# Gates of the last two tiles and x of the last loaded early, the last tiles' ends shared by ACT and DVE, and the last weight block's products put last

## The chip, the cores and the metric

The kernel runs on one core of one Trainium2 chip. The metric is the device time of one execution in microseconds (us); a number quoted for a kernel is the median of its runs. The trace of a kernel is one profiled execution; its span (first to last instruction) was 1.73 to 1.95 us shorter than the time of the same run.

Engines, as this kernel uses them (instructions on the page of the kernel before): PE multiplies matrices into PSUM banks (4674), ACT applies functions of one input (791), DVE does elementwise work on one or two inputs (833), POOL issues most loads and does a few small operations (80), SP issues transposes and the last outputs. PEld is PE's weight load (4674).

## The reference, cut to what matters

```python
xn = layernorm(x)                                   # x: (1, 2048, 448), bf16
s = attention(xn, k_cache, v_cache, wq) @ wo        # 16 heads of 256, 8 K/V heads, window 512
g = silu((gelu(xn @ w_gate) * (xn @ w_up)) @ w_down)
out = x + s * g
```

The kernel cuts the 2048 rows into 16 tiles of 128 rows, t = 0 to 15, in four chunks of four. It computes the gates g of all tiles early and parks them in DRAM (`g2d`, twice the gate: hence the factor 0.5 below). Attention then goes chunk by chunk. Each tile ends with "s times gate, plus x, write out". The ends of tiles 0 to 11 run under the attention of the following chunk. The ends of tiles 12 to 15 come when nothing else is left: this is the tail, which the change is about.

## The kernel before

A helper records operations with the buffers that they read and write and derives all semaphore waits from these. It gives each engine and each DMA issuer its list in program order, and makes a write to a buffer wait until the buffer's last readers are done.

```python
NG2 = 2      # places for gates: g2[:, t % 2]
NXR = 3      # places for x:     xr[:, t % 3]; the result is added into the same place and written out from it
CUT = D - P  # 320: tile 15 is done in two pieces, columns 0:320 and 320:448

def wo_mm(t4, b, c0=0, c1=D):                  # last four blocks (28 to 31) of s @ wo, added into the bank
    mms([(bank[b][:, c0:c1], oT[:, i, t4 * P:(t4 + 1) * P], wo[:, i - NCO + NL, c0:c1], False, i == NCO - 1)
         for i in range(NCO - NL, NCO)], b_oT[NCO - NL:] + [b_wo], (b_ps[b],))

# turn(t4, b, c0, c1): products with the identity bring the other blocks' sums into the same bank   [cut]

def wo_end(t, c0, c1, mult, bt, y):
    x, g = t % NXR, t % NG2
    bx = [b_xr[x][i] for i in range(2) if (c0 < CUT, c1 > CUT)[i]]
    mult(g2[:, g, :], b_g2[g])
    if t + NG2 < NT and c1 == D:
        load_g2(t + NG2)                       # DMA issued by POOL
    add("dve", xr[:, x, c0:c1], y[:, c0:c1], xr[:, x, c0:c1], bt + bx, bx)
    dma("sp" if t >= NT - 4 else "pool", out_view[:, t, c0:c1], xr[:, x, c0:c1], bx, ())
    if t + NXR < NT and c1 == D:
        dma("pool", xr[:, x, :], x_view[:, t + NXR, :], (), b_xr[x])

def wo_fin(c, t4, b, c0=0, c1=D):              # end of a tile of the last chunk
    ...                                        # [cut]
    def mult(g, bg):                           # tmp is 32 bit
        K.op("dve", lambda e: e.scalar_tensor_tensor(
            out=tmp[:, s, c0:c1], in0=bank[b][:, c0:c1], scalar=0.5, in1=g[:, c0:c1],
            op0=ALU.mult, op1=ALU.mult), (b_ps[b], bg), bt)
    wo_end(t, c0, c1, mult, bt, tmp[:, s, :])

# the program's end
ends = [(0, AB[2], 0, D), (1, AB[3], 0, D), (2, AB[0], 0, D), (3, AB[1], 0, CUT), (3, BB[0], CUT, D)]
for t4, b, c0, c1 in ends[:3]:
    turn(t4, b, c0, c1)
for i, (t4, b, c0, c1) in enumerate(ends):
    if i >= 3:
        turn(t4, b, c0, c1)
    wo_mm(t4, b, c0, c1)
    wo_fin(c, t4, b, c0, c1)
```

The softmax here doesn't subtract the row's maximum and nothing guards it: scores larger than these inputs give would overflow.

Of the kernel before, what the change touches and what calls it, by code (L numbers as in the profile page):

```python
# [5 lines left out]
ACT = mybir.ActivationFunctionType  # L6
ALU = mybir.AluOpType
# [161 lines left out]
def bass_recurrent_scan__sliding_block_cached__geglu_ffn__prompt_kernel(  # L169
# [12 lines left out]
    _, S, D = A_x.shape  # L182
# [5 lines left out]
    NT = S // P  # L188
# [4 lines left out]
    NCO = HD // P  # L193
# [7 lines left out]
    CUT = D - P  # L201
# [9 lines left out]
    with es:  # L211
        K = Plan(nc, es)
        base = [(nc.sbuf_base + 31) // 32 * 32]

        def place(name, shape, dt, at=None):
            size = {BF16: 2, F16: 2, F32: 4}[dt]
            for n in shape[1:]:
                size *= n
            size = (size + 31) // 32 * 32
            if at is None:  # L220
                at = base[0]
                base[0] += size
            assert at + size <= nc.sbuf_usable_end, (name, at + size, nc.sbuf_usable_end)
            return nc.alloc_sbuf_tensor_at(name, list(shape), dt, offset=at), at, at + size

        def sbuf_bufs(at, size, n):
            return [K.buf(at + i * size, size) for i in range(n)]
# [27 lines left out]
        NG2 = 2  # L255
        g2, a, _ = place("g2", [P, NG2, D], BF16)
        b_g2 = sbuf_bufs(a, D * 2, NG2)
        g2d = nc.dram_tensor("g2_all", [NT, P, D], BF16)
        b_g2d = [K.buf() for t in range(NT)]
# [7 lines left out]
        NXR = 3  # L267
        xr, a, _ = place("xr", [P, NXR, D], BF16)
        b_xr = [[K.buf(a + (i * D + lo) * 2, (hi - lo) * 2) for lo, hi in ((0, CUT), (CUT, D))] for i in range(NXR)]
        tmp, a, _ = place("tmp", [P, 2, QC], F32)  # L270
        b_tmp = [[K.buf(a + (i * QC + lo) * 4, (hi - lo) * 4) for lo, hi in ((0, CUT), (CUT, QC))] for i in range(2)]

        tmpb, _, _ = place("tmpb", [P, 2, 2 * QC], BF16, at=a)
# [10 lines left out]
        NL = 4  # L284
        wo, a, a2 = place("wo", [P, NL, D], BF16, at=rw + WAT[0] * Hq * N2 * 2)
        assert NL * D <= Hq * N2
        b_wo = K.buf(a, NL * D * 2)
# [34 lines left out]
        b_oT = sbuf_bufs(a, QC * 2, NCO)  # L322
# [8 lines left out]
        b_cc = [[K.buf(a_c + (i * 2 + j) * HC * 4, HC * 4) for j in range(2)] for i in range(4)]  # L331
        g2w, a_s, a2 = place("g2w", [P, 4, D], BF16, at=at)
        b_g2w = sbuf_bufs(a_s, D * 2, 4)
        sT, _, at = place("sT", [P, 4, 3, P], BF16, at=at)
        b_sT = [K.buf(a_s, 12 * P * 2) for k in range(3)]
        b_xs = [K.buf() for k in range(4)]
# [5 lines left out]
        bank = [pall[i // 2][:, (i % 2) * 512:(i % 2) * 512 + 512] for i in range(8)]  # L342
        b_ps = [K.buf() for i in range(8)]

        x_view = A_x.rearrange("b (t p) d -> p (b t) d", p=P)
        out_view = out.rearrange("b (t p) d -> p (b t) d", p=P)
# [8 lines left out]
        def dma(q, o, i, reads=(), writes=()):  # L355
            K.op(q, lambda e, o=o, i=i: e.dma_start(o, i), reads, writes, dma=True)  # L356
# [4 lines left out]
        def act(o, i, func, reads, writes, scale=1.0):  # L361
            K.op("act", lambda e, o=o, i=i: e.activation(o, i, func, scale=scale), reads, writes)  # L362

        def add(eng, o, x, y, reads, writes, op=ALU.add):
            K.op(eng, lambda e: e.tensor_tensor(o, x, y, op), reads, writes)  # L365

        def mms(lst, reads, writes, after=()):
            def fn(e):
                ins = None
                for (o, l, r, st, sp) in lst:  # L370
                    ins = e.matmul(o, lhsT=l, rhs=r, start=st, stop=sp, skip_group_check=True)  # L371
                return ins
            return K.op("pe", fn, reads, writes, after=after)
# [10 lines left out]
        def load_wr(q, i, j):  # L384
# [14 lines left out]
            out=ident[:, :], in_=ident[:, :], compare_op=ALU.not_equal, fill=1.0, base=0,  # L399
# [350 lines left out]
                    K.op("dve", lambda v, i=i, b=b, o=o, f=f: v.tensor_scalar(  # L750
                        o[:, i, :], bank[b], f, None, op0=ALU.mult), (b_ps[b],), (b_oT[i],))

        def wo_mm(t4, b, c0=0, c1=D):

            mms([(bank[b][:, c0:c1], oT[:, i, t4 * P:(t4 + 1) * P], wo[:, i - NCO + NL, c0:c1], False, i == NCO - 1)
                 for i in range(NCO - NL, NCO)], b_oT[NCO - NL:] + [b_wo], (b_ps[b],))

        def turn(t4, b, c0=0, c1=D):

            tok = slice(t4 * P, (t4 + 1) * P)  # L760
            lst = [(0, 0, tok, slice(0, P)), (P, 2, tok, HALF[0]), (N2, 1, tok, slice(0, P)), (N2 + P, 2, tok, HALF[1]),
                   (2 * N2, 3, slice(t4 % 2 * P, t4 % 2 * P + P), HALF[t4 // 2])]
            lst = [x for x in lst if c0 <= x[0] < c1]
            mms([(bank[b][:, lo:lo + k.stop - k.start], xs[j][:, q], ident[:, k], i == 0, False)
                 for i, (lo, j, q, k) in enumerate(lst)], b_xs + [b_ident], (b_ps[b],))

        def wo_end(t, c0, c1, mult, bt, y):

            x, g = t % NXR, t % NG2
            bx = [b_xr[x][i] for i in range(2) if (c0 < CUT, c1 > CUT)[i]]  # L770
            mult(g2[:, g, :], b_g2[g])
            if t + NG2 < NT and c1 == D:
                load_g2(t + NG2)
            add("dve", xr[:, x, c0:c1], y[:, c0:c1], xr[:, x, c0:c1], bt + bx, bx)
            dma("sp" if t >= NT - 4 else "pool", out_view[:, t, c0:c1], xr[:, x, c0:c1], bx, ())
            if t + NXR < NT and c1 == D:
                dma("pool", xr[:, x, :], x_view[:, t + NXR, :], (), b_xr[x])

        def load_g2(t):
            dma("pool", g2[:, t % NG2, :], g2d[t], (b_g2d[t],), (b_g2[t % NG2],))  # L780

        def wo_fin(c, t4, b, c0=0, c1=D):
            t = c * 4 + t4
            s = t % 2
            bt = [b_tmp[s][i] for i in range(2) if (c0 < CUT, c1 > CUT)[i]]

            def mult(g, bg):
                K.op("dve", lambda e: e.scalar_tensor_tensor(  # L788
                    out=tmp[:, s, c0:c1], in0=bank[b][:, c0:c1], scalar=0.5, in1=g[:, c0:c1],
                    op0=ALU.mult, op1=ALU.mult), (b_ps[b], bg), bt)  # L790
            wo_end(t, c0, c1, mult, bt, tmp[:, s, :])

        o_view = oTh.rearrange("p (h e) (r q) -> p e r h q", e=2, r=2)
        HALF = (slice(0, R), slice(R, P))
# [111 lines left out]
        def burst_end(c, t4):  # L906
            t = c * 4 + t4
            s, u = t % 2, t4 // 2
            y = tmpb[:, s, 0:D]

            def mult(g, bg):
                two = lambda x, lo, hi: x[:, 0:2 * N2].rearrange("p (n d) -> p n d", n=2)[:, :, lo:hi]
                for at, i, reads in ((lambda x: two(x, 0, P), sT[:, t4, 0:2, :], b_sT[:2]),
                                     (lambda x: two(x, P, N2), sT[:, t4, 2, :].rearrange("p (n d) -> p n d", n=2), b_sT[2:]),
                                     (lambda x: x[:, 2 * N2:D], sN[:, t4 % 2, u * R:u * R + R], [b_sN])):
                    add("dve", at(y), i, at(g), reads + [bg], b_tmp[s], ALU.mult)
            wo_end(t, 0, D, mult, b_tmp[s], y)
# [7 lines left out]
        for m in range(NS):  # L925
            if m in groups:
                hi = groups[groups.index(m) + 1]
# [34 lines left out]
        ends = [(0, AB[2], 0, D), (1, AB[3], 0, D), (2, AB[0], 0, D), (3, AB[1], 0, CUT), (3, BB[0], CUT, D)]  # L962
        for t4, b, c0, c1 in ends[:3]:
            turn(t4, b, c0, c1)
        for i, (t4, b, c0, c1) in enumerate(ends):
            if i >= 3:
                turn(t4, b, c0, c1)
            wo_mm(t4, b, c0, c1)
            wo_fin(c, t4, b, c0, c1)

        K.schedule()
# [53 lines left out]
```

## Time and profile before

| quantity | before |
|---|---|
| time, median of the first 3 runs (of 4, with one more beside the changed kernel) | 557.06 us (556.98 us) |
| span of the profiled run | 554.6 us |
| PE busy | 543.2 us (98%) |
| first turning product of the tail (start S) | 540.85 us |
| end of DVE's last add | 552.45 us |

The page's first part gives busy time, share of the span and number of instructions; its second part gives the busy share in 40 slices, in tenths. These are its line for all engines and its slices of PE, of the kernel before:

```profile
PE 543.2 (98%) x4674; PEld 295.0 (53%) x4674; DVE 361.3 (65%) x833; ACT 312.6 (56%) x791; POOL 41.1 (7%) x80
PE   9999999999999999999999999999999999999993
```

PE is at least 90% busy in every slice but the last. The share of 98% thus hides the end: PE's last product ends at 545.46, and others work for another 9 us. The chain of waits of that stretch (start, duration, what; lines of code by number) shows what it consists of, in the kernel before:

```profile
543.02 0.64 DVE tmp L788
...
543.94 2.48 DMA g<-g_all
...
546.51 0.64 DVE tmp L788
...
547.31 0.44 POOL xr L356
...
547.84 2.97 DMA g<-g_all
...
550.90 0.50 DVE tmp L788
...
552.16 0.29 DVE xr L365
```

The gate of tile 14 is loaded only when tile 12's multiply has freed its place. The gate of tile 15 is issued by POOL at 547.84, behind POOL's load of x for tile 15 at 547.31. The two gate loads alone are 5.45 us of the chain. The waits of that stretch (engine, output and line, what it waited for: us in all, times, longest) say the same:

```profile
DVE tmp L788 <- DMA g<-g_all: 4.1, 2, 3.1
POOL xr L356 <- DVE tmp L788: 2.8, 1, 2.8
```

The second line names a DVE multiply as what the x load waited for. The code has no such dependence: the x load takes the place that tile 12's *output* is read from, so it waits for that output to land.

The groups of instructions by form show what the arithmetic costs. First the ends in the tail, then the ends of tiles 0 to 11, which are done in 16 bit, both of the kernel before:

```profile
L788 DVE SCALAR_TENSOR_TENSOR tmp<-bank,g 128x448 f32<-128x448 f32 x3 | 1.9, 623 | 2.0 <-PE bank L371 1.0 <-DMA g<-g_all 1.0
L365 DVE TENSOR_TENSOR xr<-tmp,xr 128x448 bf16<-128x448 f32 x3 | 1.9, 625 | 0.1
```

```profile
L365 DVE TENSOR_TENSOR xr<-tmpb,xr x12: 391/392/393, 250.1 to 494.9; 128x448 bf16<-128x448 bf16 x12
```

In the tail a multiply takes 623 ns and an add 625 ns. The same add from 16-bit operands takes 392 ns (the second fence has minimum, median and maximum in ns).

### The profile page before, as it was taken

The page shows a single profiled execution, that of the slowest core. Times are in us where ns is not written, and L with a number is a line of the kernel's source. Part 1 is how long each engine was busy: PE and PEld are TensorE (multiplying, and loading weights), DVE is VectorE, ACT ScalarE, POOL GpSimd, SP SyncE. Part 2 cuts the span into 40 slices and gives each one's busy share as a digit, 9 for nine tenths or more (in the row PEclk, how much of TensorE's full clock was granted, in tenths as well). Part 3 has the DMA queues.
Part 4 walks back from the last instruction along what each step waited for, and adds up shares of the span by engine and source line. Part 5 has one row for each costly group of instructions (what it writes and reads, how often), then busy time and mean ns, then how long its engine had stood idle before and what let it go on. Part 6 is the DMA issues. An engine that isn't in the chain of part 4 may idle for free.

```text
span 554.6 us, 11965 instructions
## 1 busy us (share of the span) xinstructions
PE 543.2 (98%) x4674; PEld 295.0 (53%) x4674; DVE 361.3 (65%) x833; ACT 312.6 (56%) x791; POOL 41.1 (7%) x80
## 2 busy tenths in 40 slices
PE   9999999999999999999999999999999999999993
PEld 5554444445444444974444489444446954444781
DVE  6664635663447758856766795487578746767854
ACT  5434536763548768037857831687586058858320
POOL 1141500000000000003001000300100012010001
PEclk9999999999999999999999999999999999999997
DMA  9566399903316826424853840387176026846602
GB/s 293 127 183 143 83 274 285 157 16 91 83 32 138 154 49 155 45 31 112 155 113 85 158 95 11 75 163 161 37 152 144 7 46 153 144 84 146 125 1 60
DMA packets 177001, 63.29 MB, mean 114 GB/s; under 512 B 159808, under 2 KB 173648, under 8 KB 176944
## 3 DMA queue, kind: packets, MB, share of 16 engines
q1 hardware_dynamic: 172960, 52.76, 45.4%
q0 software_dynamic: 3216, 9.18, 5.8%
q8 instruction: 37, 0.61, 0.5%
q10 hardware_dynamic: 768, 0.57, 0.3%
q14 instruction: 20, 0.16, 0.1%
HBM read 20.22 MB, written 3.67 MB: 43 GB/s over the span
## 4 chain that ended last, share of the span: by engine, by line
PE 91%; DMA 3%; DVE 3%; ACT 2%; issue 1%; POOL 0%; DVEq 0%; POOLq 0%; ACTq 0%
PE bank L371 91%; DMA pT<-pn 2%; ACT p L724 1%; DMA g<-g_all 1%; DVE pn L731 1%; DMA x<-in_A_x_dram 0%; DVE tmp L788 0%; DVE rden L728 0%; DVE xnT L365 0%; DVE stats L418 0%; PE bank L469 0%; DVE oT L750 0%; ACT cc L362 0%; DVE xr L365 0%; DVE sr L365 0%
## 5 line engine op out<-in xcount | busy, mean ns | idle before, releaser
L724 ACT ACTIVATE p<-bank 128x512 f32<-128x512 f32 x256 | 150.5, 595 | 24.6 <-DVE pn L731 19.2
L371 PE MATMUL bank<-pT,va 128*128 128x512 bf16 x512 | 120.8, 379 | 0.4 <-DMA pT<-pn 0.4
L371 PE MATMUL bank<-kT,qT 128*128 128x512 bf16 x512 | 121.0, 379 | 0.0
L731 DVE TENSOR_SCALAR pn<-p,rden 128x512 bf16<-128x512 f32 x256 | 113.0, 484 | 9.6 <-DMA pT<-pn 5.4
L371 PE MATMUL bank<-xnT,wq 64*128 64x512 bf16 x768 | 94.9, 376 | 0.0
L371 PE MATMUL bank<-xnT,wgu 64*128 64x512 bf16 (+2 forms) x768 | 84.0, 350 | 0.1
L371 PEld LDWEIGHTS bank<-kT,qT 128*128 128x128 bf16 x512 | 49.4, 98 | 62.0 <-issue 3.8
L371 PEld LDWEIGHTS bank<-pT,va 128*128 128x128 bf16 x512 | 49.7, 98 | 61.3 <-DMA pT<-pn 2.0
L362 ACT ACTIVATE qT<-bank 128x512 bf16<-128x512 f32 x76 | 44.1, 596 | 53.2 <-PE bank L371 51.6
L709 DVE CAST qT<-bank 128x512 bf16<-128x512 f32 x52 | 35.1, 692 | 43.7 <-PE bank L371 43.7
L371 PEld LDWEIGHTS bank<-xnT,wq 64*128 64x128 bf16 x768 | 36.7, 94 | 46.3 <-ACT p L724 1.7
L371 PEld LDWEIGHTS bank<-xnT,wgu 64*128 64x128 bf16 x768 | 37.0, 94 | 36.9 <-issue 0.7
L537 DVE TENSOR_TENSOR actT<-bank,gl 128x512 bf16<-128x512 f32 x56 | 37.8, 690 | 26.5 <-PE bank L371 19.9
L362 ACT ACTIVATE gl<-bank 128x512 bf16<-128x512 f32 x56 | 33.2, 597 | 37.1 <-PE bank L371 35.0
L728 DVE RECIPROCAL rden<-rsum 128x2 f32<-128x2 f32 x128 | 21.2, 165 | 48.6 <-ACT p L724 48.4
L724 ACT ACTIVATION_READ_ACCUMULATOR p<-bank 128x1 f32 x256 | 51.4, 201 | 0.0
L371 PE MATMUL bank<-wd,actT 128*128 128x448 bf16 x224 | 43.0, 353 | 0.0
L750 DVE TENSOR_SCALAR oTh<-bank 128x512 f16<-128x512 f32 x62 | 42.4, 684 | 0.0
L371 PE MATMUL bank<-sr,wt 128*64 128x256 f16 x744 | 41.5, 273 | 0.2 <-DVE sr L365 0.2
L371 PEld LDWEIGHTS bank<-sr,wt 128*64 128x64 f16 x744 | 40.1, 110 | 1.1 <-DVE sr L365 0.5
L362 ACT ACTIVATE xnT<-bank 128x256 bf16<-128x256 f32 (+2 forms) x12 | 4.9, 417 | 63.2 <-PE bank L371 62.6
L356 POOL DMA_DIRECT2D g<-g_all x16 | 8.6, 538 | 410.6 <-DVE tmpb L365 387.3
(65 smaller groups left out, 427.3 us busy)
## 6 DMA issues: line engine op xcount, KB each, us to landing
wtb<-in_A_wo_dram POOLq DMA_DIRECT2D x4, 768.0 KB, 7.3
wq<-in_A_wq_dram SPq DMA_DIRECT2D x2, 1536.0 KB, 10.8
va<-in_A_v_cache_dram SPq DMA_DIRECT2D x8, 256.0 KB, 5.2
pT<-pn SPq DMA_TRANSPOSE x128, 2.8
g_all<-g2w SPq DMA_DIRECT2D x16, 112.0 KB, 2.0
xr<-in_A_x_dram POOLq DMA_DIRECT2D x16, 112.0 KB, 2.3
g<-g_all POOLq DMA_DIRECT2D x16, 112.0 KB, 2.3
wd<-in_B_w_down_dram SPq DMA_DIRECT2D x1, 1568.0 KB, 7.3
```

The costliest lines, as they stand in the source:

```text
L356: K.op(q, lambda e, o=o, i=i: e.dma_start(o, i), reads, writes, dma=True)
L362: K.op("act", lambda e, o=o, i=i: e.activation(o, i, func, scale=scale), reads, writes)
L371: ins = e.matmul(o, lhsT=l, rhs=r, start=st, stop=sp, skip_group_check=True)
L537: K.op("dve", lambda e: e.tensor_tensor(actT[:, c % 2, f, :], bank[b + 1], gl[:, s, :], ALU.mult), (b_ps[b + 1], b_gl[s]), (b_actT[c % 2][ ...
L709: K.op("dve", lambda v, s=s, b=b: v.tensor_copy(qT[:, s, 1, :], bank[b + 1]), (b_ps[b + 1],), (b_qT[s][1],))
L724: K.op("act", lambda e, b=b, r=r, z=z: e.activation(p32[:, z, :], bank[b], ACT.Exp, scale=att_scale, accum_out=rsum[:, r:r + 1]), (b_ps[b] ...
L728: K.op("dve", lambda e, r=r: e.reciprocal(rden[:, r - 1:r + 1], rsum[:, r - 1:r + 1]), b_rsum[r - 1:r + 1], b_rden[r - 1:r + 1])
L731: K.op("dve", lambda e, r=r - 1 + t, z=(n - 1 + t) % NP32, y=y, t=t: e.tensor_scalar(pn[:, y, t, :], p32[:, z, :], rden[:, r:r + 1], None, ...
L750: K.op("dve", lambda v, i=i, b=b, o=o, f=f: v.tensor_scalar(o[:, i, :], bank[b], f, None, op0=ALU.mult), (b_ps[b],), (b_oT[i],))
```

## The change

It has three parts.

1. **Early loads.** The gates of tiles 14 and 15 and x of tile 15 get places of their own, in a region that is free once tile 11's end is done.
2. **Ends by ACT and DVE.** For tiles 13 to 15, ACT copies the bank to a 16-bit tile (with the factor 0.5), and DVE multiplies and adds in 16 bit. Tile 12 stays as it was.
3. **Order of the products.** Blocks 28 to 30 of tiles 12 and 13 come first; block 31, whose input is ready last (PE waits 0.43 us for it in the kernel before), follows for both.

```diff
+        b_gz = sbuf_bufs(a_s, D * 2, 2)
+        b_xz = [K.buf(a_s + (2 * D + lo) * 2, (hi - lo) * 2) for lo, hi in ((0, CUT), (CUT, D))]
 ...
-        def wo_mm(t4, b, c0=0, c1=D):
+        def wo_mm(t4, b, c0=0, c1=D, lo=NCO - 4, hi=NCO):
 ...
         def wo_end(t, c0, c1, mult, bt, y):
-            x, g = t % NXR, t % NG2
+            x, bx = (xr[:, t % NXR, :], b_xr[t % NXR]) if t < NT - 1 else (g2w[:, 2, :], b_xz)
+            g, bg = (g2[:, t % NG2, :], b_g2[t % NG2]) if t < NT - 2 else (g2w[:, t % 2, :], b_gz[t % 2])
 ...
-            if t + NG2 < NT and c1 == D:
+            if t + NG2 < NT - 2:
                 load_g2(t + NG2)
 ...
+            if t == NT - 5:
+                K.reuse(b_gz + b_xz)
+                for i in range(2):
+                    dma("pool", g2w[:, i, :], g2d[NT - 2 + i], (b_g2d[NT - 2 + i],), (b_gz[i],))
+                dma("pool", g2w[:, 2, :], x_view[:, NT - 1, :], (), b_xz)
 ...  (in wo_fin)
             def mult(g, bg):
+                if t4 == 0:
+                    ...            # as before, 32 bit
+                    return
+                act(y[:, c0:c1], bank[b][:, c0:c1], ACT.Copy, (b_ps[b],), bt, scale=0.5)
+                add("dve", y[:, c0:c1], y[:, c0:c1], g[:, c0:c1], bt + [bg], bt, ALU.mult)
 ...  (at the end)
+        for t4, b, c0, c1 in ends[:2]:
+            wo_mm(t4, b, c0, c1, NCO - NL, NCO - 1)
         for i, (t4, b, c0, c1) in enumerate(ends):
 ...
-            wo_mm(t4, b, c0, c1)
+            wo_mm(t4, b, c0, c1, NCO - 1 if i < 2 else NCO - NL)
```

More of the change, by code (lines that the diff above doesn't have):

```diff
@@ L751, in pv @@
                         o[:, i, :], bank[b], f, None, op0=ALU.mult), (b_ps[b],), (b_oT[i],))
-        def wo_mm(t4, b, c0=0, c1=D):
+        def wo_mm(t4, b, c0=0, c1=D, lo=NCO - 4, hi=NCO):
             mms([(bank[b][:, c0:c1], oT[:, i, t4 * P:(t4 + 1) * P], wo[:, i - NCO + NL, c0:c1], False, i == NCO - 1)
-                 for i in range(NCO - NL, NCO)], b_oT[NCO - NL:] + [b_wo], (b_ps[b],))
+                 for i in range(lo, hi)], b_oT[lo:hi] + [b_wo], (b_ps[b],))
         def turn(t4, b, c0=0, c1=D):
@@ L767, in wo_end @@
         def wo_end(t, c0, c1, mult, bt, y):
-            x, g = t % NXR, t % NG2
-            bx = [b_xr[x][i] for i in range(2) if (c0 < CUT, c1 > CUT)[i]]
-            mult(g2[:, g, :], b_g2[g])
-            if t + NG2 < NT and c1 == D:
-                load_g2(t + NG2)
-            add("dve", xr[:, x, c0:c1], y[:, c0:c1], xr[:, x, c0:c1], bt + bx, bx)
-            dma("sp" if t >= NT - 4 else "pool", out_view[:, t, c0:c1], xr[:, x, c0:c1], bx, ())
-            if t + NXR < NT and c1 == D:
-                dma("pool", xr[:, x, :], x_view[:, t + NXR, :], (), b_xr[x])
+            x, bx = (xr[:, t % NXR, :], b_xr[t % NXR]) if t < NT - 1 else (g2w[:, 2, :], b_xz)
+            g, bg = (g2[:, t % NG2, :], b_g2[t % NG2]) if t < NT - 2 else (g2w[:, t % 2, :], b_gz[t % 2])
+            bx = [bx[i] for i in range(2) if (c0 < CUT, c1 > CUT)[i]]
+            mult(g, bg)
+            if t + NG2 < NT - 2:
+                load_g2(t + NG2)
+            add("dve", x[:, c0:c1], y[:, c0:c1], x[:, c0:c1], bt + bx, bx)
+            dma("sp" if t >= NT - 4 else "pool", out_view[:, t, c0:c1], x[:, c0:c1], bx, ())
+            if t + NXR < NT - 1:
+                dma("pool", xr[:, t % NXR, :], x_view[:, t + NXR, :], (), b_xr[t % NXR])
+            if t == NT - 5:
[3 more added lines that the diff above has]
+                dma("pool", g2w[:, 2, :], x_view[:, NT - 1, :], (), b_xz)
         def load_g2(t):
@@ L785, in wo_fin @@
             bt = [b_tmp[s][i] for i in range(2) if (c0 < CUT, c1 > CUT)[i]]
+            if t4:
+                y = tmpb[:, s, 0:D] if c0 == 0 else tmpb[:, s, CUT:CUT + D]
             def mult(g, bg):
-                K.op("dve", lambda e: e.scalar_tensor_tensor(
-                    out=tmp[:, s, c0:c1], in0=bank[b][:, c0:c1], scalar=0.5, in1=g[:, c0:c1],
-                    op0=ALU.mult, op1=ALU.mult), (b_ps[b], bg), bt)
-            wo_end(t, c0, c1, mult, bt, tmp[:, s, :])
+                if t4 == 0:
+                    K.op("dve", lambda e: e.scalar_tensor_tensor(
+                        out=tmp[:, s, c0:c1], in0=bank[b][:, c0:c1], scalar=0.5, in1=g[:, c0:c1],
+                        op0=ALU.mult, op1=ALU.mult), (b_ps[b], bg), bt)
+                    return
+                act(y[:, c0:c1], bank[b][:, c0:c1], ACT.Copy, (b_ps[b],), bt, scale=0.5)
+                add("dve", y[:, c0:c1], y[:, c0:c1], g[:, c0:c1], bt + [bg], bt, ALU.mult)
+            wo_end(t, c0, c1, mult, bt, tmp[:, s, :] if t4 == 0 else y)
         o_view = oTh.rearrange("p (h e) (r q) -> p e r h q", e=2, r=2)
```

## The prediction

> **What bounds the kernel.** The page gives a span of 554.6 us with PE busy 543.2 us (98%); the chain that ended last is 91% PE. Only the end is not: PE's slices show 9 but for the last (3). Timeline: PE's last product starts at 545.1, yet DVE works until 552.45, and the span ends 2.1 us later (last output's landing 1.5). The chain of waits from 543 us: multiply of tile 12 (0.64), gate load of tile 14 (2.48), multiply (0.64), POOL's x load issue (0.44), gate load of tile 15 (2.97), last multiplies and adds. The gate loads wait for the multiplies of tiles 12 and 13 to free their places, the second also behind the x load on POOL. DVE stands 1.0 and 3.1 us for them.
>
> **What the change does.**
> 1. *Early loads.* Gates 14, 15 and x of 15 go to a region free after tile 11's end (about 495 us), some 50 us ahead. No load is left in the tail. Alone: 543.0 + 3x1.25 (whole tiles) + 1.55 (last, in two pieces) = about 548.3 instead of 552.45: -4.1 us.
> 2. *Tiles 13 to 15 via ACT.* Now a DVE multiply out of PSUM takes 0.62 and the add with a 32-bit operand 0.62 (128x448). The 16-bit add in the earlier ends (128x448) takes 0.391. [...] So a whole tile costs DVE 0.78, not 1.25; the last pieces about 2x0.32 + 2x0.22 (estimates from 16-bit operations of 64, 128 and 448 columns), not 1.55. Saved: 3x0.47 = 1.4 us. ACT copies (256 columns 0.38, 512 columns 0.58, so about 0.54 for 448) run under DVE's previous tile; ACT is idle there.
> 3. *Last weight block last.* PE waits 0.43 us for the last oT at 541.6 to 542.05; six products (0.19 each) fill it. But tile 12's end then comes behind tile 13's first three: 543.1 instead of 542.99. PE ends 0.4 us earlier, for which nothing waits: DVE ends last. Worth 0, or -0.1 us of gain.
>
> **Sum.** Tile 12 to 544.4; 13 to 545.2; 14 to 546.0; 15 to 547.2. DVE ends 5.3 us earlier. Four outputs then leave within 3 us instead of 8, so the last may land 0 to 0.4 us slower. All of it is on the chain that ends last; the 540 us before don't change. Three POOL issues of 0.54 us move to 495 us, where PE waits for no POOL.
>
> **Time:** 557.06 - 5.2 = about 551.8 us, range 550.9 to 552.9. (-0.9%): faster by over 2% 1%, within 2% 98%, slower 1%.
>
> **What the profile would show.** No gate or x load after 520 us; DVE without a wait for a DMA in the tail; DVE end at about 547; multiplies and adds of 0.39, copies of 0.54; PE no longer waiting for oT; tile 12's multiply starting at 543.1, not earlier; the last output landing in 1.5 to 2 us. The PE stretch up to 541 us the same within 0.3 us.
>
> **What would make it wrong.** ACT's turn-around (buffers reused by parity: tile 14's copy waits for tile 12's add, tile 15's for tile 13's) becoming the chain: up to +0.6. Outputs bunching: +0.5. The early loads disturbing the transposes at 495 us: small. A different chip: 0.5.

Estimate from the trace: the multiply of a copied tile would take the 0.39 us of the 16-bit add, hence 0.78 us a tile. The sum puts DVE's end at 547.2 instead of 552.45, the 5.3 us, of which 5.2 were forecast for the time. What bunched outputs, the early loads or another chip might cost are guesses that no run had shown.

## The result, and the profile after

The changed kernel takes 551.42 us (4 runs, 550.95 to 552.08) against 556.98 us (4 runs of the kernel before). The ratio is 0.990, with a 95% interval from 0.9883 to 0.9918. A ratio in this document is the mean time of one kernel's runs over that of the other's of the same rounds, so not quite the ratio of the quoted medians. The time fell by 5.56 us between the medians, where 5.2 us was forecast.

DVE and ACT in the tail, from the timeline of the changed kernel, with SP's issue of the last two outputs (other rows are left out). A row gives start, us, engine, line, operation, output and inputs, count, idle time before and what ended it; line numbers are 2 to 11 higher than before:

```profile
544.02 0.62 DVE L799 SCALAR_TENSOR_TENSOR tmp<-bank,g 128x448 f32<-128x448 f32 x1 [0.99 <-PE bank L373]
544.21 0.54 ACT L364 ACTIVATE tmpb<-bank 128x448 bf16<-128x448 f32 x1 [1.94 <-PE bank L373]
544.68 0.62 DVE L367 TENSOR_TENSOR xr<-tmp,xr 128x448 bf16<-128x448 f32 x1
545.22 0.39 DVE L367 TENSOR_TENSOR tmpb<-tmpb,g 128x448 bf16<-128x448 bf16 x1
545.34 0.54 ACT L364 ACTIVATE tmpb<-bank 128x448 bf16<-128x448 f32 x1 [0.59 <-DVE xr L367]
545.64 0.39 DVE L367 TENSOR_TENSOR xr<-tmpb,xr 128x448 bf16<-128x448 bf16 x1
545.95 0.39 DVE L367 TENSOR_TENSOR tmpb<-tmpb,g2w 128x448 bf16<-128x448 bf16 x1
546.07 0.60 ACT L364 ACTIVATE tmpb<-bank 128x320 bf16<-128x320 f32 x2 [0.19 <-DVE xr L367]
546.37 0.39 DVE L367 TENSOR_TENSOR xr<-tmpb,xr 128x448 bf16<-128x448 bf16 x1
546.68 0.32 DVE L367 TENSOR_TENSOR tmpb<-tmpb,g2w 128x320 bf16<-128x320 bf16 x1
547.04 0.33 DVE L367 TENSOR_TENSOR g2w<-tmpb,g2w 128x320 bf16<-128x320 bf16 x1
547.28 0.22 DVE L367 TENSOR_TENSOR tmpb<-tmpb,g2w 128x128 bf16<-128x128 bf16 x1
547.39 0.90 SPq L358 DMA_DIRECT2D out_dram<-g2w  x2
547.53 0.23 DVE L367 TENSOR_TENSOR g2w<-tmpb,g2w 128x128 bf16<-128x128 bf16 x1
```

From 544.02 on DVE goes from one operation to the next without a stop. The waits for gate loads are gone, and no gate or x load is left in the tail: POOL issues the two gates at 499.31 and x of tile 15 right after, at 500.61 (the row of the gates, from POOL's timeline of the changed kernel):

```profile
499.31 1.30 POOL L358 DMA_DIRECT2D g2w<-g_all  x2
```

Each 16-bit step costs 0.39 us where a 32-bit one cost 0.62.

The starts of the tails are not equal. In the 14 profiled runs, S (the first turning product) lies between 540.85 and 542.58 us, although these kernels run the same instructions up to there, apart from three loads. The difference of 1 us between the two profiles here is built up over the whole run: the first output left at 250.9 and 251.5 us, the last early one at 495.7 and 496.5. So a span is a poor witness for a change of a few tenths, and the tails are measured from S. "DVE end" is the end of DVE's last add:

| kernel | S | DVE end after S | span's end after DVE end | sum |
|---|---|---|---|---|
| before | 540.85 | 11.60 | 2.15 | 13.75 |
| changed, first profile | 541.89 | 5.87 | 2.54 | 8.41 |
| changed, second profile (another chip) | 542.58 | 5.87 | 2.45 | 8.32 |

Spans are printed to 0.1 us, so the last two columns are good to about 0.05. The tail is 5.34 to 5.43 us shorter, which accounts for the measured 5.56 us within the scatter of the runs.

### The profile page after: what moved, and what is told of

Read it like the earlier page. It is cut to its first block, busy times and chain, and to the rows that moved or that the text cites. A ratio compares the mean times of both kernels' runs of the same rounds, so it can differ in the third digit from the quotient of the medians.

```text
span 550.3 us, 11945 instructions
## 1 busy us (share of the span) xinstructions
PE 540.5 (98%) x4649; PEld 294.7 (54%) x4674; DVE 360.0 (65%) x833; ACT 314.2 (57%) x795; POOL 41.4 (8%) x80
## 4 chain that ended last, share of the span: by engine, by line
PE 91%; DMA 2%; DVE 2%; ACT 2%; issue 1%; SPq 0%; ACTq 0%; DVEq 0%
PE bank L373 91%; ACT p L726 2%; DMA pT<-pn 2%; DVE pn L733 1%; DMA x<-in_A_x_dram 1%; DVE rden L730 0%; DVE tmpb L367 0%; SPq L358 0%; DVE qT L711 0%; DVE stats L420 0%; DVE tmp L799 0%; DVE sr L367 0%; DVE oTh L752 0%; ACT qT L364 0%; DVE g2w L367 0%
## 5 line engine op out<-in xcount | busy, mean ns | idle before, releaser
L373 PE MATMUL bank<-kT,qT 128*128 128x512 bf16 x487 | 117.8, 379 | 2.3 <-ACT qT L364 1.0
```

Source lines behind the costliest of these rows:

```text
L373: ins = e.matmul(o, lhsT=l, rhs=r, start=st, stop=sp, skip_group_check=True)
```

## The experiments

Twelve kernels were run in four groups, each beside runs of the kernel before on the same chip, with five rounds (three in the last group). All gave correct results.

| kernel | median, us | before, same rounds | ratio (95%) | S | DVE end after S | span's end after that | sum |
|---|---|---|---|---|---|---|---|
| loads_only | 552.74 | 557.19 | 0.9926 (0.9914 to 0.9938) | 541.54 | 7.29 | 2.17 | 9.46 |
| act_only | 556.72 | 557.19 | 0.9990 (0.9976 to 1.0003) | 541.12 | 10.66 | 2.52 | 13.18 |
| order_only | 557.06 | 557.19 | 0.9997 (0.9985 to 1.0010) | 541.49 | 11.59 | 2.22 | 13.81 |
| after_no_order | 551.84 | 557.19 | 0.9908 (0.9895 to 0.9922) | 541.42 | 6.14 | 2.54 | 8.68 |
| swap_only | 555.02 | 557.23 | 0.9949 (0.9934 to 0.9964) | 541.28 | 9.64 | 2.18 | 11.82 |
| after_again | 552.71 | 557.23 | 0.9908 (0.9891 to 0.9925) | 542.58 | 5.87 | 2.45 | 8.32 |
| t12_16bit_actq | 551.31 | 557.23 | 0.9885 (0.9866 to 0.9905) | 541.60 | 5.64 | 2.26 | 7.90 |
| pool_add13_actq | 552.25 | 557.23 | 0.9903 (0.9886 to 0.9919) | 541.45 | 6.27 | 2.88 | 9.15 |
| t12_16bit | 552.03 | 557.21 | 0.9909 (0.9895 to 0.9922) | 542.38 | 5.64 | 2.58 | 8.22 |
| last_whole | 551.40 | 557.21 | 0.9897 (0.9884 to 0.9911) | 541.86 | 5.49 | 2.45 | 7.94 |
| own_places_actq | 551.21 | 557.01 | 0.9887 (0.9870 to 0.9905) | 542.13 | 5.64 | 2.13 | 7.77 |
| loads_order | 552.58 | 557.01 | 0.9919 (0.9901 to 0.9936) | 540.87 | 7.26 | 2.17 | 9.43 |

### Each part alone

**loads_only** keeps part 1 and undoes the others:

```diff
 # against the changed kernel
-                act(y[:, c0:c1], bank[b][:, c0:c1], ACT.Copy, (b_ps[b],), bt, scale=0.5)
-                add("dve", y[:, c0:c1], y[:, c0:c1], g[:, c0:c1], bt + [bg], bt, ALU.mult)
+                ...                        # scalar_tensor_tensor out of the bank for all tiles [cut]
-        for t4, b, c0, c1 in ends[:2]:
-            wo_mm(t4, b, c0, c1, NCO - NL, NCO - 1)
 ...                                       # wo_mm takes all four blocks again [cut]
```

> Only the early loads of gates 14, 15 and x of 15; the ends still by DVE out of PSUM in 32 bit, products in the old order. Theory A (the late loads were the tail's chain): DVE without a wait for a DMA, one whole tile every 1.20 us as in the kernel before (543.02 to 544.22), so DVE's end moves from 552.45 to about 548.2 on the clock of before, time 3.9 to 4.3 us lower, about 552.9. Rival B (the arithmetic of the ends is what the tail waits for): gain at most 5.56 - 1.4 from multiplies and adds, but with most of the rest already lost to outputs bunching, under 3 us.

The tail's sum fell from 13.75 to 9.46 us, DVE's end by 4.31 us, and the ratio of 0.9926 is 4.1 us. Theory A's forecast held and rival B's "under 3 us" did not. DVE's rows of tile 14 and the first piece of 15 show an unbroken pace, at a step of 1.19 us (546.10 to 547.29); between tiles 12 and 13 of the kernel before it was 1.20:

```profile
546.10 0.62 DVE L796 SCALAR_TENSOR_TENSOR tmp<-bank,g2w 128x448 f32<-128x448 f32 x1
546.75 0.62 DVE L367 TENSOR_TENSOR xr<-tmp,xr 128x448 bf16<-128x448 f32 x1
547.29 0.48 DVE L796 SCALAR_TENSOR_TENSOR tmp<-bank,g2w 128x320 f32<-128x320 f32 x1
```

**act_only** is the kernel before with the changed kernel's `wo_fin` alone:

```diff
 # against the kernel before, in wo_fin; tile 12 keeps the 32-bit multiply [cut]
+                act(y[:, c0:c1], bank[b][:, c0:c1], ACT.Copy, (b_ps[b],), bt, scale=0.5)
+                add("dve", y[:, c0:c1], y[:, c0:c1], g[:, c0:c1], bt + [bg], bt, ALU.mult)
```

> Only the ends of tiles 13 to 15 by ACT and DVE in 16 bit, loads as late as before. Theory A: the last gate load still lands about 7.8 us after the start of tile 12's multiply (550.81 against 543.02 before), since it stands behind the x load that waits for tile 12's output; only the last tile's arithmetic after it shortens, 1.55 to about 0.95 us: time 0.5 to 0.7 us lower, about 556.4. Rival B (savings add up independently): the whole 1.4 us of DVE work comes off, about 555.6.

The medians differ by 0.47 us and the ratio's interval includes 1; the tail's sum fell by 0.57 us. That is theory A's size, and less than half of rival B's 1.4. The interval alone would not decide: its lower end, 0.9976, is a gain of 1.3 us. The trace does. DVE finishes tile 14 at 547.54 and then stands for three microseconds:

```profile
547.15 0.39 DVE L365 TENSOR_TENSOR xr<-tmpb,xr 128x448 bf16<-128x448 bf16 x1
550.58 0.33 DVE L365 TENSOR_TENSOR tmpb<-tmpb,g 128x320 bf16<-128x320 bf16 x1 [3.03 <-DMA g<-g_all]
```

Here time saved ahead of a wait for a DMA mostly lengthened the wait: tile 14 ended 0.52 us sooner after S than in the kernel before, but the last gate load left only 0.06 us sooner. (DVE's end itself came 0.94 us earlier, because this run's last gate load also landed faster, in 2.43 instead of 2.97 us, and the end after DVE was 0.37 us longer. The work after that load fell by 0.35 us, from 1.55 to 1.20, and not by the 0.6 expected. That the sum lies in theory A's range is thus in part luck; that the wait took up the rest is not.)

**order_only** is the kernel before with part 3 alone:

```diff
 # against the kernel before; wo_mm's new arguments [cut]
+        for t4, b, c0, c1 in ends[:2]:
+            wo_mm(t4, b, c0, c1, NCO - NL, NCO - 1)
-            wo_mm(t4, b, c0, c1)
+            wo_mm(t4, b, c0, c1, NCO - 1 if i < 2 else NCO - NL)
```

> Only the last weight block's products last. Theory A: PE ends 0.4 us earlier but tile 12's multiply starts at the same time within 0.1 us after the turning products, and with it all loads: time the same within 0.2 us (below what timing can resolve). Rival C (PE's wait for oT delays the tail): 0.4 us lower.

DVE's end after S is 11.59 against 11.60 us, and the time's interval holds 1. PE's wait for oT (0.43 us in the kernel before) is gone, but nothing came of it. Theory A held.

### Is the order worth anything inside the whole change?

**after_no_order** is the changed kernel without part 3 (the lines of order_only's diff taken away).

> The changed kernel with the products in the old order: Theory A: PE waits 0.4 us for oT again, but DVE's end relative to the first turning product is the same within 0.1 us (5.9 us), time about 551.4 to 551.7. Rival C: 0.4 us slower than the changed kernel, DVE's end at 6.3 us after the first turning product.

This is where the prediction's third step fails. DVE's end is at 6.14 us after S instead of 5.87: the order is worth 0.27 us here, outside the 0.1 us that theory A allowed. Rival C's 0.4 us is not reached either. ACT and DVE from the timeline of after_no_order show where it goes:

```profile
544.25 0.62 DVE L367 TENSOR_TENSOR xr<-tmp,xr 128x448 bf16<-128x448 f32 x1
544.35 0.54 ACT L364 ACTIVATE tmpb<-bank 128x448 bf16<-128x448 f32 x1 [2.54 <-PE bank L373]
544.92 0.39 DVE L367 TENSOR_TENSOR tmpb<-tmpb,g 128x448 bf16<-128x448 bf16 x1
...
545.17 1.29 ACT L364 ACTIVATE tmpb<-bank 128x448 bf16<-128x448 f32 x3 [0.27 <-PE bank L373]
545.35 0.39 DVE L367 TENSOR_TENSOR xr<-tmpb,xr 128x448 bf16<-128x448 bf16 x1
```

S is 541.42 here. Tile 13's copy starts 2.93 us after S; in the changed kernel it starts at 2.32 (544.21 - 541.89). So the copy ends at 544.89, and DVE, whose add ends at 544.87, starts the multiply at 544.92. In the changed kernel the multiply starts 0.08 us before the add's end (545.22 against 545.30). The multiplies of tiles 12, 13, 14 and the first piece of 15 start 0.04, 0.17, 0.26 and 0.27 us later after S than in the changed kernel. Here ACT's copies wait for PE (2.54 and 0.27 us in the rows), and DVE for the copies. The times can't show it: the intervals of all three runs overlap (0.990 and 0.9908 for the changed kernel, 0.9908 without the order).

**loads_order** asks whether the order needs the copies to be worth something. It is the changed kernel with the 32-bit ends of the kernel before:

```diff
-                act(y[:, c0:c1], bank[b][:, c0:c1], ACT.Copy, (b_ps[b],), bt, scale=0.5)
-                add("dve", y[:, c0:c1], y[:, c0:c1], g[:, c0:c1], bt + [bg], bt, ALU.mult)
+                ...                        # scalar_tensor_tensor out of the bank for all tiles
```

> Early loads and the order of the products, ends all by DVE out of PSUM in 32 bit. It tells whether the order needs ACT's copies to be worth something. If it does (the copies are what waits for PE): DVE's end at 7.25 us after the first turning product, 0.04 us less than with the early loads alone, since only tile 12's start moves. If the order pays whenever the loads are early: about 7.0 us, 0.27 us less.

DVE's end is at 7.26 us, 0.03 less than with the early loads alone. So in these runs the order paid only where ACT's copies stood between PE and DVE: with a DVE that needs 1.20 us a tile, PE was far enough ahead (in loads_only and loads_order DVE waits 1.03 and 0.99 us for PE before tile 12's multiply, and before none of the later ones). In order_only DVE waited for gates on top of that, 0.98 and 3.17 us.

### Why were the loads late: POOL's order, or the places?

**swap_only** is the kernel before with one pair of loads exchanged:

```diff
-            if t + NXR < NT and c1 == D:
+            if t + NXR < NT - 1:
                 dma("pool", xr[:, x, :], x_view[:, t + NXR, :], (), b_xr[x])
+            if t == NT - 3:                    # after the gate load of tile 15 on POOL's list
+                dma("pool", xr[:, (NT - 1) % NXR, :], x_view[:, NT - 1, :], (), b_xr[(NT - 1) % NXR])
```

> The kernel before with one thing changed: POOL issues the gate load of tile 15 ahead of the x load of tile 15; no new places. Theory D (two chains are behind the late loads: gate 15 stands behind the x load, and that waits for tile 12's output to land, since it takes its place): the gate lands about 547.4 on the clock of before instead of 550.81, but the x load still lands about 549.7, so tile 15's first add starts there and DVE ends near 550.8: time 1.4 to 1.7 us lower. Rival E (only the order on POOL is at fault): DVE goes through without a stop after 548, ends near 549.4, time about 3 us lower. Rival F (only the places are at fault): no change.

The time fell by 2.2 us between the medians, the tail's sum by 1.93. The sum beats theory D's 1.4 to 1.7 us because the x load also came 0.2 us earlier after S, and landed in 2.3 instead of 2.4 us. The form is theory D's. POOL and DVE from the timeline of swap_only:

```profile
545.56 0.54 POOL L356 DMA_DIRECT2D g<-g_all  x1 [0.66 <-DVE tmp L790]
547.51 0.54 POOL L356 DMA_DIRECT2D xr<-in_A_x_dram  x1 [1.42 <-DMA out_dram<-xr]
548.39 0.49 DVE L790 SCALAR_TENSOR_TENSOR tmp<-bank,g 128x320 f32<-128x320 f32 x1
549.91 0.49 DVE L365 TENSOR_TENSOR xr<-tmp,xr 128x320 bf16<-128x320 f32 x1 [1.03 <-DMA xr<-in_A_x_dram]
```

With the gate in time, tile 15's multiply runs at 548.39; then its add waits 1.03 us for x. Here the profile names what the x load waits for: tile 12's output, which SP had issued at 544.76, 2.75 us earlier. In the kernel before, the x load came 2.98 us after that output's issue (547.31 - 544.33), in act_only 2.92 us (547.52 - 544.60), although tile 14's multiply, which the page named, ended 0.16 us before the load in the one and 0.41 us in the other. Measured from the landing of that output (2.4 us after its issue in both, as in order_only), the x load came 0.54 to 0.55 us later in all three runs (0.28 in swap_only; why less, stays open). The label in the kernel before was thus wrong, and the place was the cause. Two chains stood behind tile 15: the gate behind POOL's list, and x behind an output. A swap cures the first; places of their own cure both.

### What bounds the new tail, and is there more?

**after_again** is the changed kernel unchanged, to stand beside the next two on their chip.

> The changed kernel once more, to stand beside the other three on the same chip: ratio to before 0.990, DVE's end 5.9 us after the first turning product, span's end 2.5 us after that.

It repeated 5.87 us for DVE's end, and 2.45 us behind it.

**t12_16bit** lets tile 12's multiply write 16 bit; **t12_16bit_actq** also issues the very last output from ACT:

```diff
-                        out=tmp[:, s, c0:c1], in0=bank[b][:, c0:c1], scalar=0.5, in1=g[:, c0:c1],
+                        out=y[:, c0:c1], in0=bank[b][:, c0:c1], scalar=0.5, in1=g[:, c0:c1],
 ...                                       # y, the 16-bit tile, for tile 12 too [cut]
 # t12_16bit_actq only
-            dma("sp" if t >= NT - 4 else "pool", out_view[:, t, c0:c1], x[:, c0:c1], bx, ())
+            dma("act" if t == NT - 1 and c0 else "sp" if t >= NT - 4 else "pool", out_view[:, t, c0:c1], x[:, c0:c1], bx, ())
```

> The changed kernel, with tile 12's multiply writing 16 bit, so that its add takes 0.39 instead of 0.62 us, and the very last output issued from ACT instead of SP. Theory G (DVE's work is now the tail's chain, and SP's second issue 0.4 us after the first is what lengthened the end): DVE's end at +5.64 instead of +5.87 us after the first turning product, the span's end 2.15 instead of 2.54 us after DVE's end: together 0.6 us lower than the changed kernel. Rival: the outputs in flight together are slow for their own sake: the end stays 2.5 us after DVE.

> The changed kernel with tile 12's multiply writing 16 bit, outputs all from SP: DVE's end at +5.64 us after the first turning product (seen with the last output from ACT); the span's end then 2.5 us later if SP's second issue 0.4 us after the first costs the end, 2.26 if leaving from ACT made no difference.

DVE's end came to 5.64 us in both, exactly the 0.23 us of one cheaper add: DVE's work is the chain of the new tail. The span's end after DVE is 2.26 us with the last output from ACT and 2.58 us without; before it was 2.15, which is what theory G expected from ACT. A later kernel with the output from ACT (own_places_actq, below) came to 2.13. But the end has more than one part. This is the time from issue to landing of the last two outputs (`--dma`):

| kernel | 80 KB | 32 KB, the last | last one issued by |
|---|---|---|---|
| before, loads_only | 1.6 | 1.5 | SP |
| act_only | 1.9 | 1.8 | SP |
| changed, both profiles | 2.0 | 1.8 | SP |
| t12_16bit | 2.1 | 1.9 | SP |
| t12_16bit_actq | 1.9 | 1.7 | ACT |
| own_places_actq | 1.9 | 1.6 | ACT |
| pool_add13_actq | 2.5 | 2.3 | ACT |

In two kernels with ACT the last output lands up to 0.2 us sooner than with SP (under 0.1 against after_again, on the same chip), yet still later than in the kernel before; in pool_add13_actq it lands later than in any other. So SP's issue is at most a part of the longer end, and the rival (outputs in flight together are slow) is not refuted. Another 0.2 us that ACT gains lies behind the landing: the span ends 0.7 us after the last landing in t12_16bit and after_again, and 0.5 us in t12_16bit_actq; why, no run shows. The rows of the last issues, first of t12_16bit and then of t12_16bit_actq, show the part that is SP's:

```profile
547.65 0.96 SPq L358 DMA_DIRECT2D out_dram<-g2w  x2
547.79 0.23 DVE L367 TENSOR_TENSOR g2w<-tmpb,g2w 128x128 bf16<-128x128 bf16 x1
```

```profile
547.01 0.23 DVE L367 TENSOR_TENSOR g2w<-tmpb,g2w 128x128 bf16<-128x128 bf16 x1
547.26 0.35 ACTq L358 DMA_DIRECT2D out_dram<-g2w  x1
```

SP ends its second issue 0.59 us after DVE's end (547.65 + 0.96 against 548.02); ACT ends its only one 0.37 us after it (547.61 against 547.24). This is one profile of each, on two chips. Between the two the issue ended 0.22 us sooner after DVE's end, and the output landed in 0.2 us less, not more. The second issue itself took 0.56 us in t12_16bit, 0.51 and 0.47 in the changed kernel's two profiles, each about 0.4 us after the first, and 0.67 in act_only; in the kernel before and in loads_only, 0.53 us after the first, it took 0.33 to 0.34. Why, no run shows.

**pool_add13_actq** goes on from t12_16bit_actq, moves one of DVE's adds to POOL, and gives tile 14's copy a place of its own (`b_yz`) while tile 15's copies use tile 12's:

```diff
-            add("dve", x[:, c0:c1], y[:, c0:c1], x[:, c0:c1], bt + bx, bx)
+            add("pool" if t == NT - 3 else "dve", x[:, c0:c1], y[:, c0:c1], x[:, c0:c1], bt + bx, bx)
-            s = t % 2
+            s = (0, 1, None, 0)[t4]
 ...                                       # b_yz and its place for tile 14's copy [cut]
```

> As the one before, and tile 13's add on POOL, with a place of its own for tile 14's copy so that it need not wait for tile 12's add. Theory G: DVE's work shrinks by one add, and PE with the copies of tile 15 becomes the chain: DVE's end at about +5.35 us, 0.3 us lower still, unless POOL's add (never measured here at this size) takes over 2 us or slows DVE's 16-bit operations while it runs.

A miss, and by the expectation's last clause. DVE's end is at 6.27 us instead of the hoped-for 5.35. The two rows that matter, of pool_add13_actq:

```profile
545.02 1.03 POOL L368 TENSOR_TENSOR xr<-tmpb,xr 128x448 bf16<-128x448 bf16 x1 [23.61 <-DVE tmpb L368]
545.10 1.19 DVE L368 TENSOR_TENSOR g2w<-g2w 128x448 bf16<-128x448 bf16 x1 [0.17 <-ACT g2w L365]
```

DVE's multiply, started while POOL's add ran, took 1.19 us instead of 0.39. Taking the add from DVE let the multiply start only 0.18 us sooner (3.65 us after S, against 3.83 in the next kernel), since it then waited for ACT's copy; so even without the stretch most of the hoped-for 0.3 us was not there. But that multiply's operands also lay in new places, so **own_places_actq** takes POOL out and leaves the places:

```diff
 # against pool_add13_actq
-            add("pool" if t == NT - 3 else "dve", x[:, c0:c1], y[:, c0:c1], x[:, c0:c1], bt + bx, bx)
+            add("dve", x[:, c0:c1], y[:, c0:c1], x[:, c0:c1], bt + bx, bx)
```

> The kernel with the add on POOL, with that add back on DVE and all else kept (places of its own for tile 14's copy, last output from ACT). It tells the two differences apart. If POOL's add is what stretched DVE's multiply of tile 14 to 1.19 us: the multiply takes 0.39 us again and DVE's end is at 5.6 to 5.7 us after the first turning product. If the new place of tile 14's operands is: the multiply stays near 1.2 us and the end near 6.4 us.

The same multiply, of own_places_actq:

```profile
545.96 0.39 DVE L368 TENSOR_TENSOR g2w<-g2w 128x448 bf16<-128x448 bf16 x1
```

It takes 0.39 us, and DVE's end is at 5.64 us again, 0.63 us sooner. It was POOL's add: beside its 1.03 us DVE's multiply took 0.80 us longer, and ended 0.24 us after it. How the one holds up the other, the traces do not show.

**last_whole** goes on from t12_16bit (outputs from SP) and does tile 15 in one piece:

```diff
-        ends = [(0, AB[2], 0, D), (1, AB[3], 0, D), (2, AB[0], 0, D), (3, AB[1], 0, CUT), (3, BB[0], CUT, D)]
+        ends = [(0, AB[2], 0, D), (1, AB[3], 0, D), (2, AB[0], 0, D), (3, AB[1], 0, D)]
```

> The same, with the last tile in one piece again (products, copy, multiply, add and output of 448 columns; the two pieces were made when an end was 1.25 us of DVE). Two DVE operations and one output fewer. Theory G: DVE's work falls by about 0.3 us, PE's last product at +4.0 us with one copy of 0.54 becomes the chain, DVE's end at about +5.36 us; one output of 112 KB lands in 1.7 to 2.0 us, so the span's end 2.3 us after DVE: 0.3 to 0.5 us lower than t12_16bit. Rival: one piece exposes the whole copy after PE's end and the larger output, no gain.

DVE's end came to 5.49 us (5.36 expected) and the sum to 7.94 us, 0.28 below t12_16bit, a little less than expected. The cut of the last tile, made for a slower end, no longer pays. The rows of last_whole show how close ACT and DVE now run:

```profile
545.96 0.54 ACT L364 ACTIVATE tmpb<-bank 128x448 bf16<-128x448 f32 x1 [0.33 <-PE bank L373]
546.11 0.39 DVE L367 TENSOR_TENSOR xr<-tmpb,xr 128x448 bf16<-128x448 bf16 x1
546.54 0.39 DVE L367 TENSOR_TENSOR tmpb<-tmpb,g2w 128x448 bf16<-128x448 bf16 x1
```

Tile 15's copy ends at 546.50, tile 14's add too, and the multiply starts at 546.54. Three kernels thus have a clearly shorter tail than the changed kernel (8.32 and 8.41 us): own_places_actq (7.77), t12_16bit_actq (7.90) and last_whole (7.94). In time, t12_16bit_actq was lower than the changed kernel on the same chip in all runs (551.19 to 551.49 against 552.07 to 552.94), but 1.0 us of that difference is where S fell in the two profiles, and the intervals of the ratios overlap. A gain of some 0.5 us is shown by the tails, not by the times.

## Why the prediction was right

The time (551.8 forecast, 551.42 measured) and the forecast gain (5.2 against 5.56) were right; at this scatter of the runs that says little of the single steps. Point by point:

1. *Early loads, -4.1 us.* Right. Alone they took 4.31 us off DVE's end and 4.29 off the tail's sum. A whole tile costs 1.20 us, not 1.25, since a multiply that didn't depend on the add before it started 0.08 us before that add's end.
2. *Ends via ACT, -1.4 us.* The size was right, with a condition that was missing. On top of the early loads this part took off 1.15 us (7.29 to 6.14), and the full 1.42 us only together with the order (5.87). Without the early loads the sum fell by 0.57 us. The durations were as forecast: 0.39 for multiply and add, 0.54 for a copy, 0.32 and 0.22 for the pieces.
3. *Last block last, "Worth 0, or -0.1 us of gain".* Wrong in size and sign: inside the whole change it is worth 0.27 us, without ACT's copies 0.03 (loads_order) or nothing (order_only). The step that failed is "PE ends 0.4 us earlier, for which nothing waits: DVE ends last". That an engine ends last doesn't mean that nothing else on the way is waited for: ACT's copies wait for PE, and DVE for the copies. The prediction had listed ACT's turn-around as a risk but not tied it to the order. Nor did tile 12's multiply start later (2.13 us after S, against 2.17 before): the products begin 0.60 us after S, while the sum had let them start only at the end of the turning products' row, 0.77 us after S.
4. *Outputs landing 0 to 0.4 us slower.* Right in size: the span's end moved from 2.15 to 2.45 and 2.54 us after DVE's end, the last output's landing from 1.5 to 1.8 us after its issue. The reason given, "four outputs then leave within 3 us", is not shown. In act_only only the last two outputs were in flight together, and they landed as late (1.9 and 1.8 us). What the late cases share is that the last two issues lie 0.40 us apart instead of 0.53. With the last one issued from ACT at most 0.2 us of the landing came back, not all, and pool_add13_actq landed latest (2.3), though its outputs leave no closer together than the changed kernel's (tiles 13 to 15 within 1.7 us in both). How much is SP's issue and how much the outputs on their way together stays open.
5. *DVE's end 5.3 us earlier.* Measured from S it was 5.73 us. The 0.4 us more came from point 3 and from overlaps of DVE's operations; part was given back under point 4.
6. *"The PE stretch up to 541 us the same within 0.3 us."* Wrong: S came 1.04 us later, so DVE's end stood at 547.76 and not at 547.2. Since S lies anywhere between 540.85 and 542.58 over these kernels, and the time fell by as much as the tail did, the runs do not lay this on the change.

Step 2's estimate held: for 128x448 DVE took 385 to 392 ns with both operands in bf16 out of SBUF (multiply and add of the changed kernel), against 623 ns with a PSUM operand and 625 ns with a 32-bit one (the kernel before). In the columns alone the difference was a factor of two: between 128x448 and 128x128 the multiply differed by 340 ns out of PSUM (623 and 283) and by 166 ns in 16 bit (385 and 219).

## What to carry to other kernels

When the page says 98% busy, look at the last slice: the tail has its own chain, and loads that waited there for a freed place stood in it with their whole round trip (2.48 and 2.97 us for the two gates), so give the last tiles places of their own as soon as any region falls free. Do the loads first and the arithmetic after, since most of the arithmetic saved in front of a late load was lost here (1.4 us of DVE work was worth at most 0.57 us without the loads), and a part that is worth nothing alone can be worth something once the others have moved the chain (the order: 0.01 us of DVE's end alone, 0.27 inside the change). Check a named releaser against the code, and before moving work from DVE to POOL measure what POOL's operation does to DVE's (1.19 us instead of 0.39 here).
